# Eight stores of normalised rows moved behind the first block's last gradient store, and the next row tiles loaded one row pair later

## Chip, cores and metric

The kernel runs on one core of a Trainium2 chip. The metric is the device time of one execution in microseconds (us). Engines are named as the profile names them: PE is the matrix engine (its weight loads are PEld), DVE the vector engine, ACT the scalar engine, POOL GpSimd, and SP the engine that issues most of the DMAs. "SPq" marks what SP issues. The clock granted to PE is 1.00 over the whole profile of the kernel before.

## What is computed

The reference is the forward and backward pass of a sum of two branches over a normalised input. With x of 2048 rows by 1024 columns and weights of 1024 by 3584:

```python
xn = layernorm(x)                                   # rows, eps 1e-5
A  = xn * (conv_over_2048_rows(k_shift * v, ssm_k) + k_shift * v * ssm_D)
B  = (relu(xn @ W_gate) * (xn @ W_up)) @ W_down
out = x + A + B
# and the gradients of x, k, v, shift_k, ssm_k, ssm_D, W_gate, W_up, W_down for a given grad_out
```

For branch B the backward pass needs grad_out @ W_down^T (`ps_h` in the kernel), the gradients of gate and up (`ug_d`), and then the weight gradients and the gradient of xn. Everything is bf16 with f32 sums.

## The kernel before, in words

The kernel is one instruction stream per engine, ordered partly by hand and partly by a planner that places each instruction by a priority and by its dependencies. `keep_in_program_order` (through `Pri.pin`, line 32) fixes an instruction's place on its engine. `issue_after(ins)` lets an instruction be placed on its queue only behind another one. Neither adds a wait of its own in the running program.

**Phases.** `hidden` (line 1223) makes gate, up and grad_out @ W_down^T; `grad_down` (1621) and `grad_in` (1660) make the weight gradients; `out_phase` (1709) and `grad_x` (1825) finish the outputs. Beside `hidden` and the weight gradients the convolution branch (`ABranch`) is woven in, a few matrix instructions at a time (`ps_c`, line 83).

**hidden.** The loop over n has 14 passes: 2 halves of 8 row tiles of 128 rows (s = 0 to 7), each against 7 column blocks of 512. A pass is called a block here: the *first block* is n = 0, the second is n = 1. In a block, the row tiles go in pairs (sp = 0, 2, 4, 6). For a pair there are two products for gate (`ps_g`), two for up (`ps_u`) and two for the gradient (`ps_h`), each of eight 128x512 matmuls (`gemm8`, 1151). ACT takes the Relu of gate into a tile `ru` (1281), DVE multiplies with up (1296 or 1299), forms `ht` (1305), and after ACT has copied `ps_h` (1456) DVE makes both gradients in `ru` (1457). `ht` is stored to `h_d` (1310) and `ru` to `ug_d` (1462). `ru` tiles come from a ring of six buffers, `ht` and `gh` from another ring of six, and PSUM has eight banks (`open_left`, 888).

**Weights.** A block needs gate (`wg`), up (`wu`) and transposed down weights (`wdT`), four pieces of 256 KB each. The next block's pieces are loaded while a block runs, into buffers that the present block has finished with (`load_gate`, `load_up`, `load_down`, 1246 to 1267). In the first block `load_gate` runs twice, two pieces at a time. `wdT` comes through a transposing DMA (`row_piece_T`, 1169). All of these go through SP, which issues in order.

**Normalising.** The rows of x are normalised in chunks (`LN_CHUNKS`, 939): tiles 0 to 7 are read by loads 0 to 5, tiles 8 to 15 by loads 6 to 9, two row tiles (512 KB) each. The tiles lie in a ring of five buffers (`a.lnx`, 127), so load 6 overwrites the buffer that holds the normalised rows 0 and 1, load 7 that of row 2, load 8 that of row 3, and load 9 that of rows 4 and 5. Each normalised row tile is stored to `xn_d` (256 KB). The generator `layer_norm` (958) is advanced by `next(ln)`; `chunk()` (1486) advances it by three, which is one of loads 6 to 9 normalised and stored. For rows 0 to 7 the stores are not issued at once: `kept` collects them (1003, 1031) in the order of rows 0, 1, 3, 2, 4, 5, 6, 7, and lines 1526 to 1529 issue the first four behind pair sp = 2 of the first block and the other four behind pair sp = 6. Rows 8 to 15 are stored as soon as they are scaled (line 1001).

**Queues.** In the first block the stores of `h_d` and `ug_d` go through POOL (`nc.gpsimd`), as all `xn_d` stores do; from the second block on `h_d` and `ug_d` go through SP. POOL also makes the index tables for the convolution (`tables`, 149; the last of them is line 226, read by DVE at 227). In the built program the DMAs of SP rotate over eight semaphores and those of POOL over eight others, so each DMA waits until the one eight before it on its side has landed.

**The convolution branch** reads `xn_d` first at line 302 (`load_xn`, issued through line 99 by SP, in fixed order), and that load waits for all sixteen `xn_d` stores, because it reads a column slice of every row.

Of the kernel before, what the change touches and what calls it, by code (L numbers as in the profile page):

```python
# [17 lines left out]
P = 128  # L18
# [30 lines left out]
class ABranch:  # L49
# [47 lines left out]
    def load(self, out, in_):  # L97
        self.pri.now()
        ins = self.nc.sync.dma_start(out=out, in_=in_)
        if self.pin:  # L100
            self.tc.keep_in_program_order(ins)
        else:
            self.pri.pin(ins)
# [776 lines left out]
class LnMlp:  # L880
# [342 lines left out]
    def hidden(self, first, goT, load, ln, tables, Wg, Wu, Wd, g, xn_d, h_d, ug_d):  # L1223
# [6 lines left out]
        for n in range(N):  # L1230
            half, fb = divmod(n, self.FB)
            s0, cols, ahead = half * HS, slice(fb * 512, fb * 512 + 512), n == 0
# [13 lines left out]
            def load_gate():  # L1246
                if last:
                    self.slab_part(h_d, 0, "hs", self.hs, 4, sg)
                elif ahead and nw[0] is None:
                    nw[0] = self.col_block(Wg, nb, "wg", to[0], part=range(2))  # L1250
                    nw.append(self.pieces)
                elif ahead:
                    self.col_block(Wg, nb, "wg", to[0], part=range(2, 4), out=nw.pop())
                else:
                    nw[0] = self.col_block(Wg, nb, "wg", to[0])
# [5 lines left out]
            def load_down(q):  # L1261
                if last and q == 0:
                    self.slab_part(h_d, 0, "hs", self.hs, 0, spare)
                elif not last:
                    if q == 0:
                        nw[2] = []
                    nw[2].append(self.row_piece_T(Wd, nb, "wdT", to[2], q, n == 1))
# [105 lines left out]
            def gate_up(sp):  # L1373
                end = sp == HS - 2
                if ahead and not end:
                    gate(sp)
                    yield from step(self.PACE[0])

                    def turn():
                        flip(sp + 2)  # L1380
                        with self.tc.issue_after(self.copied.ins):
                            chunk()
                    up(sp, None, {4: turn})
                    yield from step(self.PACE[1])
                    gate(sp + 1)
                    yield from step(self.PACE[0])
                    up(sp + 1)
                    yield from step(self.PACE[1])
                    return
                rows = [(f, s) for f in (gate, up) for s in (sp, sp + 1)]  # L1390
                for f, s in sorted(rows, key=lambda r: r[1]) if ahead else rows:
                    f(s)
                    yield from step(self.PACE[f is up])
                    if end and f is gate and s == sp + 1:
                        (load_up if ahead else load_gate)()
                if end and ahead:
                    for q in range(4):
                        load_down(q)
                elif end:
                    load_up()  # L1400
                if swap:
                    next_rows(sp)
# [8 lines left out]
            def last_rows(sp):  # L1411

                self.hold = self.busy = True
                for q in range(2):
                    load_down(sp // 2 + q)

                def run(f, s):
                    f(s)
                    yield from step(self.PACE[f is up])
                yield from run(gate, sp)  # L1420
                yield from run(gate, sp + 1)
                yield from run(up, sp)
                yield from run(gate, sp + 2)
                yield from run(gate, sp + 3)
                load_gate()
                yield from run(up, sp + 1)
                yield from grad_row(sp)
                yield from run(up, sp + 2)
                yield from run(up, sp + 3)
                load_up()  # L1430
                self.busy = swap and not last
                if n == 1:
                    chunk()
                if swap:
                    next_rows(sp)
                    next_rows(sp + 2)
                for s in range(sp + 1, HS):
                    yield from grad_row(s)
                if swap:
                    next_grads(sp)  # L1440
                    next_grads(sp + 2)
# [7 lines left out]
            def grad_row(s, after={}):  # L1449
                ps = self.ps_tile("ps_h")  # L1450
                self.gemm8(ps, gT[s], wd, None, after)

                def finish():
                    gh = self.e1_tile("gh")
                    kept = dict(always=ahead and s == 0)
                    self.pri.pin(nc.scalar.copy(out=gh[:], in_=ps[:]), **kept)  # L1456
                    self.pri.pin(nc.vector.tensor_tensor(out=ru[s][:], in0=ru[s][:], in1=gh[:].rearrange(
                        "p (o f) -> p o f", o=1).to_broadcast([P, 2, 512]), op=ALU.mult), **kept)

                    def store(r=(s0 + s) * P, cols=cols, t=ru[s]):  # L1460
                        queue = nc.gpsimd if n == 0 else nc.sync
                        self.put = queue.dma_start(out=ug_d[r:r + P, :, cols], in_=t[:])
                        self.pri.pin(self.put)
                    self.defer(store)
                if ahead and s == 0:
                    late.append(finish)
                else:
                    finish()
                yield 1730
                self.tick()  # L1470
# [8 lines left out]
            def grad(sp):  # L1479
                for s in (sp, sp + 1):  # L1480
                    at = 3 if sp == 0 else 0
                    yield from grad_row(s, {at: lambda: flip_ahead(sp)} if ahead and s == sp + 1 else {})
                if swap:
                    next_grads(sp)
# [12 lines left out]
            for sp in range(0, HS, 2):  # L1497
                self.pri.now()
                while len(gT) < min(sp + 4, HS):
                    with self.tc.issue_after(self.turned.ins if sp == 4 else self.copied.ins):  # L1500
                        gT.append(self.load_T(g, len(gT), "goT", HS + len(gT)))
                if ahead and sp == 4:
                    with self.tc.issue_after(self.loaded.ins):
                        load_gate()
                if ahead or sp < HS - 4:
                    if not ahead:
                        load_down(sp // 2)
                        yield from gate_up(sp)
                        if n == 4 and sp == 2:
                            for k in filter(self.bare, range(HS)):  # L1510
                                xT[k] = self.load_T(xn_d, k, "xnT", k)
                        if sp:
                            self.hold = False
                        elif fb:
                            self.busy = False
                    if not ahead or sp != 4:
                        yield from grad(sp)
                    if ahead and sp == 2:
                        yield from grad(4)
                elif sp == HS - 4:  # L1520
                    yield from last_rows(sp)
                if ahead:
                    with self.tc.issue_after(self.stored.ins):
                        if sp == 0:
                            load_gate()
                if ahead and sp in (2, 6):
                    with self.tc.issue_after(self.put.ins):
                        for put in self.kept[0:4] if sp == 2 else self.kept[4:8]:
                            put()
                if ahead and sp == 6:  # L1530
                    with self.tc.issue_after(self.sent.ins):
                        load(6)
                if ahead and sp + 4 < HS:
                    yield from gate_up(sp + 4)
                if n == 1 and sp < 4:
                    with self.tc.issue_after(self.stored.ins):
                        for i in ((7,), (8, 9))[sp // 2]:
                            load(i)
                if n == 1 and sp != 4:
                    chunk()  # L1540
                if ahead and sp == 4:
                    with self.tc.issue_after(self.ln_act.ins), self.tc.issue_after(self.ln_dve.ins):
                        tables()
# [477 lines left out]
```

## Time and profile before

| | us |
|---|---|
| three runs | 1851.29, 1855.92, 1854.02 |
| their median | 1854.02 |
| the profiled execution | 1851.31 |
| its span, first to last instruction | 1849.5 |
| PE busy in the span | 1843.3 |
| DVE, ACT, POOL busy | 1118.4, 647.3, 35.0 |
| mean DMA rate over the span | 187 GB/s |

All times of rows below are us from the start of that span. A row of the timeline gives start, duration, engine, source line, operation, output and inputs, how many instructions were merged into it, and in brackets the idle time before it with what ended it. PE rows overlap a little, since a matmul's row of 0.38 us includes its way through the array, while one starts every 0.216 us. DMA rows are the time that the issuing engine spent on issuing, not the transfer.

### The profile page before, as it was taken

Reading aid. Unit: us, or ns where it says so; the run is one execution under the profiler, and the core shown is the slowest. Engines: PE = TensorE matmul, PEld = TensorE weight load, DVE = VectorE, ACT = ScalarE, POOL = GpSimd, SP = SyncE. Lnnn points to the kernel's source line nnn. Section 1 sums busy time; section 2 is a strip of 40 time slices with the busy share of each in tenths; the row PEclk is TensorE's granted clock in tenths of the full one; section 3 lists DMA queues with packets and bytes.
Section 4 is the critical chain, followed back from the end, with each engine's and each line's share of the span. In section 5 each row is a group of like instructions: output and inputs, shape, how many; then the busy total and the mean of one; then the engine's idle time right before and its main releaser. Section 6 shows DMA issues by size and latency. Waiting matters only on the chain.

```text
span 1849.5 us, 32388 instructions
## 1 busy us (share of the span) xinstructions
PE 1843.3 (100%) x13182; PEld 847.7 (46%) x13182; DVE 1118.4 (60%) x1652; ACT 647.3 (35%) x1218; POOL 35.0 (2%) x72
## 2 busy tenths in 40 slices
PE   9999999999999999999999999999999999999999
PEld 5444444444444444444444444444444544444444
DVE  6656797698789758585685667821212222566652
ACT  6644544445444454545544454320000000111100
POOL 2200000000000000000000000000000000000000
PEclk9999999999999999999999999999999999999999
DMA  9997769968767866639567445389999767799963
GB/s 251 273 219 195 172 167 240 209 168 205 186 157 199 243 162 160 166 102 273 130 155 173 142 117 161 105 232 251 256 239 249 181 144 170 173 210 215 207 150 74
DMA packets 749989, 345.97 MB, mean 187 GB/s; under 512 B 581272, under 2 KB 718480, under 8 KB 749840
## 3 DMA queue, kind: packets, MB, share of 16 engines
q1 hardware_dynamic: 736048, 312.18, 71.1%
q10 hardware_dynamic: 9632, 17.04, 3.0%
q0 software_dynamic: 4160, 14.68, 2.4%
q8 instruction: 103, 1.69, 0.4%
q14 instruction: 46, 0.38, 0.1%
HBM read 143.79 MB, written 103.83 MB: 134 GB/s over the span
## 4 chain that ended last, share of the span: by engine, by line
PE 99%; DMA 1%; DVE 0%; issue 0%; DVEq 0%
PE ps_x L1870 21%; PE ps_w L1571 20%; PE ps_h L1153 10%; PE ps_g L1153 10%; PE ps_u L1153 10%; PE ps_o L1738 10%; PE ps_d L1571 9%; PE ps_c L83 4%; PE ps_d L1587 2%; PE ps_w L1587 1%; PE ps_r L1772 0%; DMA wdT<-in_B_W_down_dram 0%; DMA wu<-in_B_W_up_dram 0%; PE ps_g L1327 0%; PE ps_u L1327 0%; PE pst_x L1198 0%
## 5 line engine op out<-in xcount | busy, mean ns | idle before, releaser
L1571 PE MATMUL ps_w<-ugs,xn_nat 128*128 128x512 bf16 x1728 | 381.1, 379 | 0.0
L87 ACT CAST arena<-ps_c 128x512 bf16<-128x512 f32 x576 | 293.8, 611 | 103.8 <-PE ps_c L83 103.6
L1153 PEld LDWEIGHTS <-xnT 128*128 128x128 bf16 x1760 | 168.7, 98 | 205.8 <-issue 6.2
L1571 PEld LDWEIGHTS <-xn_nat 128*128 128x128 bf16 x1728 | 165.4, 98 | 200.7 <-issue 6.1
L343 DVE STREAM_TRANSPOSE arena<-arena 128x1024 f32<-128x1024 f32 x96 | 179.4, 1934 | 112.2 <-ACT arena L87 101.8
L1153 PE MATMUL ps_h<-wdT,goT 128*128 128x512 bf16 x896 | 203.6, 379 | 1.5 <-DMA wdT<-in_B_W_down_dram 1.5
L1153 PE MATMUL ps_u<-wu,xnT 128*128 128x512 bf16 x880 | 202.8, 379 | 0.4 <-DMA wu<-in_B_W_up_dram 0.3
L1153 PE MATMUL ps_g<-wg,xnT 128*128 128x512 bf16 x880 | 201.6, 379 | 0.0
L1870 PE MATMUL ps_x<-wgT,ggT 128*128 128x512 bf16 x896 | 198.6, 379 | 0.0
L1870 PE MATMUL ps_x<-wuT,guT 128*128 128x512 bf16 x896 | 198.6, 379 | 0.0
L1888 ACT ACTIVATE w<-xn,m 128x512 f32<-128x512 bf16 x32 | 24.3, 807 | 480.4 <-DVE m L1881 367.0
L1738 PE MATMUL ps_o<-wd,hT 128*128 128x512 bf16 (+1 forms) x896 | 187.6, 372 | 0.0
L1571 PE MATMUL ps_d<-g_nat,hs 128*128 128x512 bf16 x768 | 169.9, 379 | 0.0
L1870 PEld LDWEIGHTS <-guT 128*128 128x128 bf16 x896 | 87.7, 98 | 105.7
L1870 PEld LDWEIGHTS <-ggT 128*128 128x128 bf16 x896 | 87.7, 98 | 105.5
L1153 PEld LDWEIGHTS <-goT 128*128 128x128 bf16 x896 | 86.7, 98 | 105.9 <-issue 2.8
L1738 PEld LDWEIGHTS <-hT 128*128 128x128 bf16 x896 | 87.7, 98 | 100.0
L1456 ACT CAST gh<-ps_h 128x512 bf16<-128x512 f32 x112 | 66.2, 593 | 184.6 <-PE ps_h L1153 174.1
L1574 ACT CAST wi<-ps_w 128x512 bf16<-128x512 f32 x108 | 64.5, 598 | 187.6 <-PE ps_w L1571 154.9
L1730 DVE TENSOR_TENSOR ya<-ya,xe 128x1024 bf16<-128x1024 bf16 x16 | 11.1, 692 | 175.1 <-DMA xe<-xn_d 175.1
L91 DVE TENSOR_TENSOR t<-arena 128x2048 bf16<-128x2048 bf16 x96 | 113.9, 1219 | 0.4
L1571 PEld LDWEIGHTS <-hs 128*128 128x128 bf16 x768 | 73.3, 98 | 88.3 <-issue 1.8
(152 smaller groups left out, 1426.8 us busy)
## 6 DMA issues: line engine op xcount, KB each, us to landing
ugs<-ug_d SPq DMA_DIRECT2D x112, 256.0 KB, 5.0
ug_d<-ru SPq DMA_DIRECT2D x104, 256.0 KB, 4.2
wu<-in_B_W_up_dram SPq DMA_DIRECT2D x56, 256.0 KB, 4.8
hs<-h_d SPq DMA_DIRECT2D x56, 256.0 KB, 4.9
out_dram<-wi SPq DMA_DIRECT2D x56, 256.0 KB, 4.5
wg<-in_B_W_gate_dram SPq DMA_DIRECT2D x55, 256.0 KB, 4.1
h_d<-ht SPq DMA_DIRECT2D x104, 128.0 KB, 2.0
gt<-in_grad_out_dram SPq DMA_DIRECT2D x32, 256.0 KB, 5.6
```

What stands on the lines that cost most here:

```text
L83: self.pri.pin(self.nc.tensor.matmul(out, lhsT=lhsT, rhs=rhs, start=start, stop=stop))
L87: self.pri.pin(self.nc.scalar.copy(out=out, in_=in_))
L91: self.pri.pin(self.nc.vector.tensor_tensor(out=out, in0=in0, in1=in1, op=op))
L343: self.pri.pin(self.nc.vector.transpose(out=df[:, c0:c0 + 32, :], in_=sf[:, c0:c0 + 32, :]))
L1153: self.pri.pin(self.nc.tensor.matmul(ps[:], lhsT=xT[:, kt * P:(kt + 1) * P], rhs=w(kt), start=(kt == 0), stop=(kt == self.DT - 1)), always ...
L1456: self.pri.pin(nc.scalar.copy(out=gh[:], in_=ps[:]), **kept)
L1571: self.pri.pin(self.nc.tensor.matmul(ps[:], lhsT=lhsT(st), rhs=rhs(st), start=(st == 0), stop=(st == self.ST - 1)))
L1574: self.pri.pin(self.nc.scalar.copy(out=out, in_=ps[:]))
L1587: self.pri.pin(self.nc.tensor.matmul(ps[i][:], lhsT=lhsT(i, st), rhs=rhs(i, st), start=(st == 0), stop=(st == self.ST - 1)))
L1738: nc.tensor.matmul(ps, lhsT=hT[:, kt, :], rhs=self.wd[:, kt, oc], start=(kt == 0), stop=(kt == self.FT - 1))
L1870: nc.tensor.matmul(ps, lhsT=T[:, kt, :], rhs=W[:, kt, oc], start=(i == 0), stop=(i == n - 1))
L1888: nc.scalar.activation(out=w[:, oc], in_=xn[:, oc], func=ACT.Identity, scale=m[:, 7:8], bias=m[:, 6:7])
```

## The change

Four edits, all in `hidden`:

1. The first four stores of normalised rows (rows 0, 1, 3, 2) no longer go out behind pair sp = 2 of the first block. All eight kept stores are issued together, behind pair sp = 0 of the second block, and placed behind the last gradient store of the first block on POOL.
2. Load 6 leaves the end of the first block. It goes where load 7 was; load 7 goes where load 8 was, and loads 7, 8 and 9 share the second place.
3. The four chunks of normalising that were called in the second block behind pairs 0, 2, 6 and inside the last pairs are now called behind pair 2, inside the last pairs, behind pair 6, and behind pair 0 of the third block.
4. The name `first_put` takes the place of `put` for the store that the kept stores go behind.

```diff
                     def store(r=(s0 + s) * P, cols=cols, t=ru[s]):
                         queue = nc.gpsimd if n == 0 else nc.sync
-                        self.put = queue.dma_start(out=ug_d[r:r + P, :, cols], in_=t[:])
-                        self.pri.pin(self.put)
+                        put = queue.dma_start(out=ug_d[r:r + P, :, cols], in_=t[:])
+                        self.pri.pin(put)
+                        if n == 0:
+                            self.first_put = put
                     self.defer(store)
...
-                if ahead and sp in (2, 6):
-                    with self.tc.issue_after(self.put.ins):
-                        for put in self.kept[0:4] if sp == 2 else self.kept[4:8]:
+                if (n, sp) == (1, 0):
+                    with self.tc.issue_after(self.first_put.ins):
+                        for put in self.kept:
                             put()
-                if ahead and sp == 6:
-                    with self.tc.issue_after(self.sent.ins):
-                        load(6)
                 if ahead and sp + 4 < HS:
                     yield from gate_up(sp + 4)
                 if n == 1 and sp < 4:
                     with self.tc.issue_after(self.stored.ins):
-                        for i in ((7,), (8, 9))[sp // 2]:
+                        for i in ((6,), (7, 8, 9))[sp // 2]:
                             load(i)
-                if n == 1 and sp != 4:
+                if (n, sp) in ((1, 2), (1, 6), (2, 0)):
                     chunk()
```

In the built program the order of PE's 26366 instructions is the same before and after. On POOL four stores move down past two `h_d` stores, five table instructions and the last two `ug_d` stores of that block. On SP one 512 KB load moves from ahead of the second block's first `wdT` issue, and the following three shift one place each. On DVE and ACT one chunk's instructions move down by one row pair or more, and the last table's two DVE instructions move behind the first gradient product of the second block.

## The prediction

> **What bounds the kernel now.** First the page: busy times, then the chain of work that ended last.
>
> ```profile
> span 1849.5 us, 32388 instructions
> PE 1843.3 (100%) x13182; PEld 847.7 (46%) x13182; DVE 1118.4 (60%) x1652; ACT 647.3 (35%) x1218; POOL 35.0 (2%) x72
> ...
> PE 99%; DMA 1%; DVE 0%; issue 0%; DVEq 0%
> ```
>
> PE is busy for 1843.3 of 1849.5 us. All that any reordering can win is the other 6.2 us, and part of that is the head and the tail. So the next view is what PE waited for:
>
> ```profile
> PE ps_h L1153 <- DMA wdT<-in_B_W_down_dram: 1.5, 1, 1.5
> PE ps_warm L1214 <- DVE warm L1211: 1.0, 1, 1.0
> PE ps_u L1153 <- DMA wu<-in_B_W_up_dram: 0.3, 1, 0.3
> ```
>
> Columns: total us, times, longest. Two waits for weights, 1.5 and 0.3 us, no wait for ACT or DVE but the warm-up's. The timeline and the chain of waits give their places, and what SP and POOL issued ahead of the first:
>
> ```profile
> 42.01 1.20 POOL L1031 DMA_DIRECT2D xn_d<-ln_x  x2
> 43.09 0.65 POOL L1001 DMA_DIRECT2D xn_d<-ln_x  x1
> ...
> 43.62 0.65 POOL L1031 DMA_DIRECT2D xn_d<-ln_x  x1
> 43.72 3.57 SPq L1144 DMA_DIRECT2D wu<-in_B_W_up_dram  x4
> ...
> 47.38 8.48 SPq L1171 DMA_TRANSPOSE wdT<-in_B_W_down_dram  x4
> ...
> 55.02 2.60 POOL L1001 DMA_DIRECT2D xn_d<-ln_x  x4
> ...
> 59.86 2.32 PE L1153 MATMUL ps_h<-wdT,goT 128*128 128x512 bf16 x10 [1.50 <-DMA wdT<-in_B_W_down_dram]
> ```
>
> ```profile
> 54.38 5.44 DMA wdT<-in_B_W_down_dram
> ```
>
> The second block's first gradient product uses the four `wdT` pieces in turn and stops before the fourth. That piece was issued at 54.38 and landed 5.44 later, at 59.82. PE wanted it at 59.86 - 1.50 = 58.36. It is 1.5 us late.
>
> **The change part by part.** *The four stores taken from 42 to 44 us.* They are 4 x 256 KB = 1.05 MB. What they cost the transfers beside them is in the DMA view of 42 to 50 us (8 us):
>
> ```profile
> q0 software_dynamic: 521, 1.70, 55.6%
> q1 hardware_dynamic: 1592, 1.17, 48.9%
> ...
> xn_d<-ln_x POOLq DMA_DIRECT2D x4, 256.0 KB, 6.0
> wu<-in_B_W_up_dram SPq DMA_DIRECT2D x4, 256.0 KB, 7.0
> ```
>
> Columns of a queue: packets, MB, share of the sixteen engines' time. q0 carries POOL's DMAs, q1 SP's. Together they take 104.5% (packets overlap a little), so the DMA engines are full, and q0's 1.70 MB took 0.556 x 8 = 4.45 us. The moved 1.05 MB is 4.45 x 1.05 / 1.70 = 2.75 us of all engines. Without it the `wu` pieces (7.0 us to land) and the `wdT` pieces behind them move up, by 2.75 us at most.
>
> How much of this reaches the fourth piece depends on its issue. The issues of the first two and of the last two pieces, from the view of this tile:
>
> ```profile
> L1171 SPq DMA_TRANSPOSE wdT<-in_B_W_down_dram x1: 2491/2491/2491, 47.4 to 47.4; - x1
> ```
>
> ```profile
> L1171 SPq DMA_TRANSPOSE wdT<-in_B_W_down_dram x1: 2654/2654/2654, 50.0 to 50.0; - x1
> ```
>
> ```profile
> L1171 SPq DMA_TRANSPOSE wdT<-in_B_W_down_dram x2: 1485/1530/1576, 52.7 to 54.4; - x2
> ```
>
> While the stores drained an issue took 2.5 to 2.7 us, afterwards 1.5 to 1.6. I read the longer ones as back-pressure from the full engines. Ends: if the long issues belong to the transposes themselves nothing moves (0); if both fall to the later pace, each saves about 1.0, so the fourth is issued 1.0 + 1.1 = 2.1 us sooner, at 52.3, and lands by 57.7 (52.3 + 5.44), ahead of the 58.36. Half of that would already take 1.05 of the 1.50 us away. I take the whole wait: **-1.5 us**, between 0 and -1.5. Two reasons: the issues speed up in this very trace as soon as the stores are through, and the landing itself (5.44) gets shorter too with less ahead of it. What comes next is no DMA wait: the block's later gradient products use the same four pieces.
>
> *The eight stores from 55 us.* The first four of the batch go out at the time, and at the pace, at which four already went; the other four follow from about 57.6 us, when the fourth piece has, by the above, all but landed. So they cost that piece nothing; if it is not early, they are no worse for it than the four before. On POOL the batch holds up one table instruction, the last `iota`:
>
> ```profile
> 57.18 0.62 POOL L226 IOTA itB<- 128x32 int32 x1
> ...
> 58.30 0.29 DVE L227 TENSOR_SCALAR itB<-itB,kkB,obB 128x32 int32<-128x32 int32 x1
> ...
> 61.10 0.69 DVE L1457 TENSOR_TENSOR ru<-ru,gh 128x1024 bf16<-128x1024 bf16 x1 [0.53 <-ACT gh L1456]
> 62.01 3.62 PE L1153 MATMUL ps_g<-wg,xnT 128*128 128x512 bf16 x16
> ```
>
> At 2.60 / 4 = 0.65 us a store the batch ends at 55.0 + 8 x 0.65 = 60.2 and the `iota` at 60.8; DVE's line 227, now placed behind the gradient product of 61.10 (59.6 without the wait), then waits some 0.5 us. PE doesn't feel that: it has eight banks, and 8 x 1.73 = 13.8 us of matrix work before it needs one back (3.62 us is the row of two products, which take 3.45 of PE's time).
>
> *Load 6 and SP.* Load 6 now waits for the stores of rows 0 and 1, since it overwrites their buffer.
>
> ```profile
> 59.89 2.04 SPq L1310 DMA_DIRECT2D h_d<-ht  x2
> 62.02 0.40 SPq L951 DMA_DIRECT2D ln_x<-in_A_q_dram  x1
> 62.52 0.67 SPq L1462 DMA_DIRECT2D ug_d<-ru  x1
> ...
> 79.48 0.60 ACT L1281 ACTIVATE ru<-ps_g 128x512 bf16<-128x512 f32 x1 [0.20 <-PE ps_g L1153]
> ```
>
> ```profile
> DMA to landing us min/median/max: 3.2/5.8/9.8
> ```
>
> The last row is for all `xn_d` stores. Row 1 goes out at 55.7 and lands at 61.5 (median) or 65.5 (longest). SP comes to load 6 at 62.0, or 60.5 without PE's wait, and stands there 1.0 us, at most 5. Queued behind it are the `ug_d` stores of the second block's first rows, a `wdT` piece for the third block, and `h_d` stores. The first to miss them is the Relu of row 6 at 79.48, which rewrites row 0's `ru` (ring of six): 62.52 + 0.67 + 5.8 = 69.0, so 10 us of slack. Cost 0.
>
> *Chunks one row pair later.* ACT and DVE lose a chunk at 65 to 73 us and gain one at about 104 to 113. ACT has four passes, about 5 us with their read-outs, in front of two Relus there; PE's list of waits names neither engine, and the 13.8 us of banks are the cover. If that cover were gone it would be under 5 us. Cost 0.
>
> *The last two stores of rows, beside the other wait.* They leave 102.45 for about 112:
>
> ```profile
> 102.45 1.07 POOL L1001 DMA_DIRECT2D xn_d<-ln_x  x2 [8.66 <-DVE ln_x L998]
> ...
> 112.92 0.69 DVE L1457 TENSOR_TENSOR ru<-ru,gh 128x1024 bf16<-128x1024 bf16 x1 [1.14 <-ACT gh L1456]
> ...
> 120.87 1.88 SPq L99 DMA_DIRECT2D xt<-xn_d  x2
> ...
> 126.38 2.83 SPq L1144 DMA_DIRECT2D wg<-in_B_W_gate_dram  x4
> ```
>
> ```profile
> 136.35 1.96 SPq L1144 DMA_DIRECT2D wu<-in_B_W_up_dram  x4
> ```
>
> ```profile
> 141.29 3.01 PE L1153 MATMUL ps_u<-wu,xnT 128*128 128x512 bf16 x12 [0.35 <-DMA wu<-in_B_W_up_dram]
> ```
>
> ```profile
> q0 software_dynamic: 160, 0.52, 14.3%
> ```
>
> The last row is the DMA view of 102 to 112 us: the two stores took 14.3% of 10 us, 1.4 us of all engines. From 113 to 138 us SP issues one DMA after the other, up to the `wu` for which PE waits 0.35 us at 141. The 1.4 us now fall in this stretch. Ends: -0.35 (the wait goes) and +1.4 (all of it is pushed through). I take **+0.4**: PE's 1.5 us move SP's stretch forward with it, as its transfers are released by PE and DVE, and a part of the 1.4 finds room.
>
> **Sum.** 1851.31 (the profiled execution: span 1849.5 and 1.8 around it) - 1.5 + 0.4 = 1850.2. The median of the runs shown lies 2.7 above the profiled one; on it the same -1.1 gives **1852.9 us**.
>
> **Rivals.**
> *A. The wait for the fourth piece stays,* because a transpose's issue has its own pace under any load. For it: the issues of 47.4 and 50.0 are alike although the mixture beside them changes. Against: those of 52.7 and 54.4. Then 0 + 0.4, or no change at all: **1854.0**.
> *B. Slower: SP stands at `xt`.* That load (120.87, or 119.4 with PE's gain) waits for every store of rows. The last two go out at about 112.1 to 112.5, behind line 998, which stands just ahead of the DVE row of 112.92, taken with PE's gain. A landing of up to 6.9 us costs nothing. At the longest seen, 9.8, SP stands for 2.9 us, in the stretch without slack, and the `wu` at its end is later by as much: with the 1.4 us of engine time it is +4.3, less 1.5: +2.8. It decides against the change from a landing of about 8.4 us, where 1.5 are used up. Central price +2.5 against -1.5: **1855.0**.
> *C. Slower: the `iota` behind the eight stores.* If POOL's stores are drawn out by the busy DVE, DVE stands at line 227, ACT at the table's sine behind it, and PE stops when the banks are full, at about 62.0 + 13.8 = 75.8. It decides from (75.8 - 0.6 - 55.0) / 8 = 2.5 us a store. The rows of the stores speak against it, with DVE little busy (42 to 45 us) and hardly ever idle (56 to 60.5 us):
>
> ```profile
> L1031 POOL DMA_DIRECT2D xn_d<-ln_x x3 | 1.8, 654 | 0.0
> ```
>
> ```profile
> L1001 POOL DMA_DIRECT2D xn_d<-ln_x x3 | 2.1, 898 | 0.0
> ```
>
> ```profile
> 51.66 1.93 POOL L209 IOTA itNi<- 128x32 int32 x1
> ```
>
> The means are 654 and 898 ns: at 0.9 the batch ends at 62.2. For it speaks only the last row, an `iota` that took 1.93 us where the one at 57.18, of the same size, took 0.62. Drawn out by the same 3.1, a store takes 2.8 us, the `iota` ends at 55.0 + 22.4 + 0.6 = 78.0 and PE stops for 2.2 us: -1.5 + 2.2 = +0.7, **1854.7**.
> The Trainium skill, "SBUF — State Buffer", section "A bandwidth-pool intuition that's wrong (but worth ruling out)", speaks for C: GpSimd can't write its DMAs' descriptors while DVE holds the port that they share, so a DMA of about 620 ns takes about 3100 ns beside a DVE copy. By that figure, as an estimate, the batch would take 24.8 us. The trace agrees with the 620 ns (654) and not with the 3100 (898).
>
> **How the numbers follow.** Forecast 0.58, A 0.22, B 0.16, C 0.04. The forecast's own range is -1.85 to -0.1 (both waits gone; half the saving and all 1.4 pushed through is near 0): 1852.2 to 1853.9. The runs shown scatter from 1851.29 to 1855.92, more than any case moves them. So the range runs from the lowest run less both waits, 1851.29 - 1.85 = 1849.4, to the highest and B's price, 1855.92 + 1.0 = 1856.9. By over 0.3% (5.6 us, about what a measurement of this kernel can tell from no change) none of the cases moves it: a gain of 5.6 would need nearly all of PE's 6.2 idle us, so faster 0.02; slower 0.03, B or C at several times its price; the same 0.95.
>
> **What would show it.** Right: in the changed profile the waits of PE have no `wdT` row, or one under 0.5 us; the four `wdT` issues from 47 us take under 2 us each; SP shows a short wait at load 6 and PE none. A: the 1.5 us row is still there. B: the wait for `wu` near 140 us is over 2 us and SP waits at line 99 for `xn_d`. C: DVE waits for POOL at line 227 for over 10 us. I am wrong outright if PE's busy time changes by more than 1 us, or if PE waits anywhere after 150 us, where nothing but the order of the moved instructions could have been passed on.

## The result and the profile after

| | before | after |
|---|---|---|
| median of nine runs each, us | 1853.25 (1849.15 to 1856.16) | 1848.77 (1848.40 to 1849.70) |
| ratio of the times, 95% interval | | 0.9977 (0.9967 to 0.9988) |
| the profiled execution, us | 1851.31 | 1848.82 |
| its span | 1849.5 | 1847.0 |

The change makes the kernel faster by 0.23% (0.12 to 0.33%). 1848.77 lies 0.63 us below the range forecast, and 4.1 below the predicted 1852.9. On the profiled executions the difference is 2.5 us, on the medians 4.5: six of these nine runs of before took over 1852 us, and none of after did.

The page of after, its span and its busy times:

```profile
span 1847.0 us, 32177 instructions
...
PE 1827.6 (99%) x12970; PEld 847.1 (46%) x13182; DVE 1118.6 (61%) x1652; ACT 646.7 (35%) x1218; POOL 34.8 (2%) x72
```

PE's busy time seems to have fallen by 15.7 us. It has not: 212 matmul records are missing (12970 beside 13182 weight loads, and before had 13182 of both). What PE waited for, after:

```profile
PE ps_w L1570 <- issue: 2.9, 18, 0.2
PE ps_d L1570 <- issue: 1.9, 12, 0.2
PE ps_warm L1214 <- DVE warm L1211: 1.0, 1, 1.0
...
PE pst_x L1198 <- DVE ln_x L1009: 0.4, 1, 0.4
PE ps_w L1586 <- DMA out_dram<-wo: 0.2, 1, 0.2
```

The many "issue" gaps of 0.2 us, all behind 600 us, are the places of missing records, and so is the one put down to `wo`: each is 0.16 to 0.18 us long, the weight loads of the missing matmuls are there, and the profiles without missing records have no such gap. The `wdT` and the `wu` rows are gone. The timeline of after at the place of the change, the DMA view of 42 to 50 us, and the issues of the `wdT` pieces:

```profile
43.52 1.94 SPq L1144 DMA_DIRECT2D wu<-in_B_W_up_dram  x4
...
45.56 8.80 SPq L1171 DMA_TRANSPOSE wdT<-in_B_W_down_dram  x5
...
56.71 3.62 PE L1153 MATMUL ps_h<-wdT,goT 128*128 128x512 bf16 x16
56.96 2.56 POOL L1001 DMA_DIRECT2D xn_d<-ln_x  x4
...
59.10 0.60 POOL L226 IOTA itB<- 128x32 int32 x1
...
59.85 1.06 SPq L951 DMA_DIRECT2D ln_x<-in_A_q_dram  x1
...
60.16 3.62 PE L1153 MATMUL ps_g<-wg,xnT 128*128 128x512 bf16 x16
...
117.71 1.32 SPq L99 DMA_DIRECT2D xt<-xn_d  x2
...
134.51 3.63 PE L1153 MATMUL ps_g<-wg,xnT 128*128 128x512 bf16 x15
...
141.72 1.09 PE L83 MATMUL ps_c<-arena,FW 64*32 64x128 bf16 x96
```

```profile
q1 hardware_dynamic: 2343, 1.75, 83.1%
q0 software_dynamic: 208, 0.66, 21.8%
...
wu<-in_B_W_up_dram SPq DMA_DIRECT2D x4, 256.0 KB, 5.1
```

```profile
L1171 SPq DMA_TRANSPOSE wdT<-in_B_W_down_dram x1: 1387/1387/1387, 45.6 to 45.6; - x1
L1171 SPq DMA_TRANSPOSE wdT<-in_B_W_down_dram x1: 2942/2942/2942, 47.0 to 47.0; - x1
L1171 SPq DMA_TRANSPOSE wdT<-in_B_W_down_dram x2: 1254/1332/1411, 50.1 to 51.4; - x2
```

POOL's queue moves 0.66 MB in these 8 us (before: 1.70), SP's 1.75 (before: 1.17). The `wu` issues take 1.94 us in place of 3.57, the pieces land after 5.1 us in place of 7.0, and the fourth `wdT` piece is issued at 51.42, 2.96 us sooner than at 54.38 (the fifth of the five belongs to the third block). So the gradient product runs through in one row of 16.

Where the 2.5 us came from is read off the starts of rows that both traces have. The first `ps_g` row of before, at 62.01, stands in the prediction; the later two rows of before are:

```profile
136.37 3.63 PE L1153 MATMUL ps_g<-wg,xnT 128*128 128x512 bf16 x16
...
144.23 1.09 PE L83 MATMUL ps_c<-arena,FW 64*32 64x128 bf16 x96
```

The first `ps_g` row moved from 62.01 to 60.16 (-1.85), the later one, ahead of the `wu` wait, from 136.37 to 134.51 (-1.86), and the `ps_c` row behind that wait from 144.23 to 141.72 (-2.51); the span's end moved by -2.5. At 7.5 us, the second `pst_x` row already stood 0.19 earlier, ahead of anything changed (7.49 and 7.30). So about 0.2 belongs to the head, 1.66 to the wait for `wdT` (1.50 of idle time and 0.16 more around it), 0.66 to the wait for `wu` at 141 us, and nothing to the 1700 us after that.

### The profile page after: what moved, and what is told of

It is laid out like the page before. It is cut to its first block, busy times and chain, and to the rows that moved or that the text cites. A ratio compares the mean times of both kernels' runs of the same rounds, so it can differ in the third digit from the quotient of the medians.

```text
span 1847.0 us, 32177 instructions
## 1 busy us (share of the span) xinstructions
PE 1827.6 (99%) x12970; PEld 847.1 (46%) x13182; DVE 1118.6 (61%) x1652; ACT 646.7 (35%) x1218; POOL 34.8 (2%) x72
## 4 chain that ended last, share of the span: by engine, by line
PE 97%; DMA 1%; issue 1%; SPq 0%; ACT 0%; DVE 0%; DVEq 0%; ACTq 0%
PE ps_x L1869 21%; PE ps_w L1570 20%; PE ps_h L1153 10%; PE ps_o L1737 10%; PE ps_u L1153 10%; PE ps_g L1153 10%; PE ps_d L1570 9%; PE ps_c L83 4%; PE ps_d L1586 1%; PE ps_w L1586 0%; DMA vt<-in_A_v_dram 0%; PE ps_r L1771 0%; DMA wu<-in_B_W_up_dram 0%; DMA out_dram<-wo 0%; DMA out_dram<-gv 0%
## 5 line engine op out<-in xcount | busy, mean ns | idle before, releaser
L1570 PE MATMUL ps_w<-ugs,xn_nat 128*128 128x512 bf16 x1675 | 375.2, 379 | 4.7 <-issue 2.9
```

The source lines that it names most:

```text
L1570: self.pri.pin(self.nc.tensor.matmul(ps[:], lhsT=lhsT(st), rhs=rhs(st), start=(st == 0), stop=(st == self.ST - 1)))
```

## Experiments

**Theory 1:** the 1.05 MB of early stores makes the fourth `wdT` piece late, and that wait is the gain; the kernel before also scatters for this reason. **Rivals:** the later place of load 6 or of the chunks carries the gain; or the scatter of before has another cause, and the gain on the profiled execution is all there is. In all kernels below PE's matrix instructions stand in the order of before, but for the extra ones that are named. Each set of runs has its own runs of the kernel before on the same chip.

### Stores alone, loads and chunks alone, and both kernels again

`e4_before_again` is the kernel before, unchanged.

> The kernel before, unchanged, to see its scatter and another of its executions. Theory 1 (the four early stores make the fourth transposed weight piece of the second block late, by an amount that differs from execution to execution): times again spread over several us, 1849 to 1856, and the profile shows the wait of PE at line 1153 for the weights near 58 us with another length than 1.5 us, while PE idles nowhere else by over 0.5 us after 10 us. Rival (the variable time sits elsewhere, near 120 to 145 us, where the convolution starts): the wait near 58 us is again 1.5 us and what differs lies at the load of the up weights near 141 us. If neither: times within 1 us of each other.

Measured: 1850.43 us (1849.27 to 1851.77, 12 runs). The 35 runs of before that go with this set had a median of 1850.46. The profile of this execution: PE's waits and the fourth piece.

```profile
PE ps_h L1153 <- DMA wdT<-in_B_W_down_dram: 1.5, 1, 1.5
```

```profile
59.30 2.32 PE L1153 MATMUL ps_h<-wdT,goT 128*128 128x512 bf16 x10 [1.55 <-DMA wdT<-in_B_W_down_dram]
```

The wait for `wdT` is there again with the same size. The wait for `wu` at 141 us is not: no row names it. It belongs to one execution, not to the kernel. And the usual time of before is 1850.4, not 1853 or 1854.

`e1_stores_only` moves only the stores: all eight behind the last pair of the first block.

```diff
-                if ahead and sp in (2, 6):
+                if ahead and sp == 6:
                     with self.tc.issue_after(self.put.ins):
-                        for put in self.kept[0:4] if sp == 2 else self.kept[4:8]:
+                        for put in self.kept:
```

> The four early stores go out with the other four, at the end of the first block; loads 6 to 9 and the chunks of normalising stay in their old places (two of the second block's stores pass load 6 on SP, as it now waits for the rows). Theory 1: the whole gain, 1848.5 to 1850.0, spread under 1.5 us, no wait for weights near 58 us. Rival 2 (load 6, sent at 56 us, is what makes the piece late): as before, about 1853 with several us of spread. Rival 3 (the gain comes from the chunks one row pair later, at 65 to 145 us): 1851 to 1853.

Measured: 1853.7 us (1852.8 to 1855.44), ratio 1.0013 (1.0005 to 1.0022). Slower, a miss. The timeline:

```profile
59.64 0.73 SPq L951 DMA_DIRECT2D ln_x<-in_A_q_dram  x1
...
73.67 2.15 SPq L1310 DMA_DIRECT2D h_d<-ht  x2
...
87.44 2.83 SPq L1144 DMA_DIRECT2D wg<-in_B_W_gate_dram  x4
...
94.18 3.03 PE L1153 MATMUL ps_g<-wg,xnT 128*128 128x512 bf16 x12 [1.41 <-DMA wg<-in_B_W_gate_dram]
97.82 0.61 PE L1153 MATMUL ps_u<-wu,xnT 128*128 128x512 bf16 x2 [0.61 <-DMA wu<-in_B_W_up_dram]
```

The wait for `wdT` is gone, as theory 1 wants, but PE now waits 1.4 us for `wg` and 1.5 us (0.61 of it in the last row) for `wu` of the third block. Load 6 goes out at 59.64, in before at 56.0; the chunk that reads it stands where it stood, so DVE comes to its passes late, SP stands at two `h_d` stores that DVE has not yet made (73.67; 70.62 in before), and the `wg` behind them in SP's order is issued at 87.44 in place of 84.64. The stores by themselves remove one wait and make another; no run of the 12 was under 1852.8 us.

`e2_loads_chunks_only` is the other part: loads and chunks as in after, stores as in before.

```diff
-                if ahead and sp == 6:
-                    with self.tc.issue_after(self.sent.ins):
-                        load(6)
...
-                        for i in ((7,), (8, 9))[sp // 2]:
+                        for i in ((6,), (7, 8, 9))[sp // 2]:
...
-                if n == 1 and sp != 4:
+                if (n, sp) in ((1, 2), (1, 6), (2, 0)):
```

> Loads 6 to 9 and the chunks later, as in the changed kernel; the eight stores in their old places. Theory 1: as before, 1853 with a spread of several us, the wait near 58 us still there. Rivals 2 and 3: the whole gain, 1848.5 to 1850.0, with little spread.

Measured: 1849.91 us (1848.88 to 1857.76), ratio 0.9993 (0.9981 to 1.0005). No change that can be told, and the wait is still there:

```profile
60.16 2.32 PE L1153 MATMUL ps_h<-wdT,goT 128*128 128x512 bf16 x10 [1.94 <-DMA wdT<-in_B_W_down_dram]
```

`f3_stores_and_chunks` is `e1` with the chunks one row pair later, and load 6 left at the end of the first block.

> As the run with the stores alone moved, but the chunks of normalising one row pair later too; load 6 stays at the end of the first block. With the stores alone, PE waited 2.9 us near 93 to 101 us for gate and up weights, since load 6 came late, the first chunk held DVE, and SP stood behind DVE. Theory 1: with the chunks later nothing stands behind load 6, and the time is that of the changed kernel, 1848.3 to 1850.0. If it is the order on SP around load 6 that costs (two stores pass it): 1853 to 1854 as with the stores alone.

Measured: 1848.71 us (1848.33 to 1851.83), ratio 0.9989 (0.9980 to 0.9998): the time of after. `f1_after_again`, the changed kernel in the same set of runs:

> The changed kernel, unchanged, again beside the kernel before. In the executions seen so far the kernel before has most times near 1850.4 us and about a third of them at 1852.6 to 1857.7 us; the changed one had nine between 1848.4 and 1849.7. Theory 1 (two effects: the wait of 1.5 us for the weights goes in every execution, and the late executions go with the early stores): all runs within 1848.3 to 1850.0, none above 1852. Rival (the late executions come from the state of the chip, and have nothing to do with the change): a fifth or more of these runs above 1852 too.

Measured: 1848.85 us (1848.49 to 1850.16), ratio 0.9986 (0.9977 to 0.9995); no row for `wdT` or `wu`. The gain is 0.14% here and was 0.23% above, since six of these 24 runs of before took over 1852 us, and six of nine above. So two edits carry the whole gain: the stores take the wait away, the later chunks keep the stores from making a new one. The place of load 6 shows no effect of its own, and the rival that gave it or the chunks the gain falls with `e2`.

### The bytes put back, and doubled

`e3_after_extra_stores` is after with four additional 256 KB stores, to a scratch tensor that nobody reads, where the four stores went out in before. `f2_before_double_stores` is before with four such stores behind the four early ones.

```diff
+                if ahead and sp == 2:
+                    with self.tc.issue_after(self.first_put.ins):
+                        for i, x in enumerate(self.kept_x[0:4]):
+                            nc.gpsimd.dma_start(out=self.scratch[i * P:(i + 1) * P, :], in_=x)
```

> The changed kernel with four additional stores of the same size (1 MB) from the same tiles at the old place, behind pair 2 of the first block, into a scratch buffer that nobody reads. Theory 1: the gain is lost, about 1853 with a spread of several us, and the wait near 58 us is back. If the place of the loads or of the chunks is what matters: 1848.5 to 1850 as in the changed kernel.

Measured: 1850.3 us (1849.48 to 1855.3), ratio 1.0001 (0.9991 to 1.0011). Timeline:

```profile
41.81 2.25 POOL L1534 DMA_DIRECT2D scratch<-ln_x  x4
43.52 3.98 SPq L1147 DMA_DIRECT2D wu<-in_B_W_up_dram  x4
47.59 9.14 SPq L1174 DMA_TRANSPOSE wdT<-in_B_W_down_dram  x5
...
58.90 2.32 PE L1156 MATMUL ps_h<-wdT,goT 128*128 128x512 bf16 x10 [0.73 <-DMA wdT<-in_B_W_down_dram]
```

The bytes alone bring back the slow `wu` issues (3.98; 1.94 in after), the wait, and the time of before. The wait is 0.73 and not 1.5 us here; this execution, at 1849.48, was the fastest of the twelve.

> The kernel before with four more stores of 256 KB, into a scratch buffer that nobody reads, right behind the four early ones. Theory 1: the wait for the fourth piece near 58 us grows from 1.5 us by up to the 2.75 us that 1 MB of stores took of all DMA engines, to 2.5 to 4.3 us: 1851.5 to 1853.5 in the common executions, and more late ones. If the piece's issue has its own pace and the stores' amount does not matter: the wait stays at 1.5 us and the time at 1850.4.

Measured: 1856.21 us (1854.74 to 1857.31, 8 runs), ratio 1.0027 (1.0017 to 1.0038). More than expected. PE's waits, and its stretch by 2 us (columns: us, busy with count, granted clock as a share of PE's full clock, DMA share, GB/s):

```profile
PE ps_h L1156 <- DMA wdT<-in_B_W_down_dram: 3.2, 2, 1.7
PE ps_u L1156 <- DMA wu<-in_B_W_up_dram: 0.7, 2, 0.5
```

```profile
60.00:62.00 2.00, 0.59 (x2) 0.83 1.14 323
62.00:64.00 2.00, 1.62 (x4) 0.50 0.84 164
64.00:66.00 2.00, 2.00 (x6) 0.50 1.16 327
66.00:68.00 2.00, 2.00 (x7) 0.50 1.06 391
```

The waits grew to 3.9 us. What was not expected is the clock: it is halved from behind 61 us to 68 us, 6.8 us in all, and 6 or 7 matmuls run in 2 us where after runs 10 or 11. That costs another 3.4 us.

### Why the kernel before scatters

`f4_before_look` is one more execution of the kernel before, and was one of its long ones.

> Another look at the kernel before. If it is one of its late executions (over 1852 us), theory 1 has the additional time as a longer wait for the fourth transposed piece near 58 us; a rival (found with the stores alone moved) has it as waits for gate and up weights at 93 to 101 us, behind a late load 6, with the wait at 58 us unchanged. If it is a common one (about 1850.4 us): one wait of 1.5 us and no other over 0.6 us after 10 us.

Measured: 1854.38 us. The timeline, the chain, and PE's stretch:

```profile
57.81 0.59 PE L1153 MATMUL ps_h<-wdT,goT 128*128 128x512 bf16 x2 [0.38 <-DMA wdT<-in_B_W_down_dram]
...
62.21 3.88 PE L1153 MATMUL ps_h<-wdT,goT 128*128 128x512 bf16 x10 [3.81 <-DMA wdT<-in_B_W_down_dram]
```

```profile
54.73 7.44 DMA wdT<-in_B_W_down_dram
```

```profile
58.00:60.00 2.00, 0.40 (x2) 1.00 1.20 138
60.00:62.00 2.00, 0.00 (x0) 1.00 1.05 212
62.00:64.00 2.00, 1.79 (x5) 0.50 1.02 394
64.00:66.00 2.00, 2.00 (x8) 0.65 1.18 350
66.00:68.00 2.00, 2.00 (x11) 1.00 1.32 366
```

The fourth piece was issued only 0.35 us later than in the profile of before, but took 7.44 us to land in place of 5.44. PE stood for 3.81 us, and then the clock was halved for 3.4 us: 4.2 us of waits less the usual 1.5, and 1.7 for the clock, are 4.4, and 1850.4 + 4.4 = 1854.8, near the 1854.38 measured. The other waits that the expectation named at 93 to 101 us are not there.

The Trainium skill, "TensorE: Matmul & The Clock Gate", section "HAM oscillation — how this bites in real kernels", names this: "no PE-idle gaps >~3.4µs", or the array falls back to half its clock. This trace agrees (a gap of 3.81 us, then 3.4 us at 0.50). `f2` doesn't: its longest gap was 1.75 us.

Each run's record has its mean granted clock, and 3.4 us at half clock show in it as 0.999. So the runs without a profile can be sorted, too, though for them the longer wait is not seen, only the clock. Of 96 runs of the kernel before beside the experiments, 73 have a clock of 1.000: 1848.72 to 1852.75 us, median 1850.34. The other 23 have 0.999 or 0.998: 1852.62 to 1857.71, median 1854.20. Under 1.000 are also 2 of the 12 runs of `e2`, 3 of 12 of `e3`, 8 of 12 of `e1` (with its own waits), and one of 11 of `f3` (1851.83). All 20 runs of after have 1.000. In the three runs shown ahead of the prediction two were over 1853.

Whether the clock falls because PE stands, or beside it because of the full DMA engines, was tried by giving PE something to do. `g2_before_filled` (and again `g5`) puts 7 matmuls, into a bank that nobody reads, ahead of the fourth piece: additional work of 1.5 us.

```diff
+                if (n, s) == (1, 0):
+                    pf = self.ps_tile("ps_fill")
+
+                    def fill(m):
+                        for _ in range(m):
+                            self.pri.pin(nc.tensor.matmul(pf[:], lhsT=gT[0][:, 0:P], rhs=gT[0][:, 0:512],
+                                                          start=True, stop=True), always=True)
+                    after = {5: lambda: fill(7)}
                 self.gemm8(ps, gT[s], wd, None, after)
```

> The kernel before with 7 extra 128x512 matmuls (1.5 us of PE's time, into a bank that nobody reads) ahead of the second block's fourth weight piece, where PE waits 1.5 us. Theory 1: in most executions the time is as before, about 1850.4 us (within 0.5), since the matmuls take the place of the wait; the late executions (one in four of before's at 1853 to 1858) had a wait of near 3.8 us and 3.4 us of half clock behind it; with 1.5 us of that filled the clock stays, so a late one is at most 2.7 us over the others, 1853.1. Rival 1: late executions come as often and as high as in before, for a reason that has nothing to do with PE standing idle. Rival 2: the matmuls add their 1.5 us in full: 1851.9.

> The same kernel again as the one before with 7 extra matmuls ahead of the fourth weight piece (1850.64 us; all 12 runs at a mean clock of 1.000, one of them at 1854.66 us), for more runs. Theory 1: again no run, or at most one, with a clock under 1.000, where 19 of 78 runs of the kernel before have one. Rival: about one in four, three of twelve.

Measured: 1850.64 us (1850.04 to 1854.66, 12 runs), ratio 0.9997 (0.9988 to 1.0005), and 1850.44 us (1850.17 to 1854.35, 11 runs), ratio 0.9998 (0.9989 to 1.0007). The first one's timeline:

```profile
58.09 1.67 PE L1456 MATMUL ps_fill<-goT 128*128 128x512 bf16 x7
59.85 2.32 PE L1153 MATMUL ps_h<-wdT,goT 128*128 128x512 bf16 x10
```

The 1.5 us of extra work cost nothing, since PE would have stood. All 23 runs have a clock of 1.000. At 23 of 96 some 5.5 were due, and the chance of none is (73/96) to the power of 23, 0.002. The 12 runs of `e4` all have 1.000 too; with them it is 85 of 108, and 0.004. Both take the runs as independent. Two of the 23 were still long (1854.66, 1854.35), above the 1853.1 expected at most, with the full clock; they have no profile, and their cause stays open.

`g1` puts 8 and 7 matmuls into `f2`, but behind the second and third pieces, so behind the wait for the second piece, the longest; `g4` puts 11 and 4 ahead of them (`after = {1: lambda: fill(11), 3: lambda: fill(4)}`); `g3` is `f2` again.

> The kernel before with the four extra scratch stores, unchanged, on the same chip as the one with the 15 matmuls, to compare with it: 1856.2 us again (1854.7 to 1857.3), with two PE waits of 1.4 to 1.8 us and half the granted clock for some us behind them.

Measured: 1856.77 us (1855.47 to 1858.23, 8 runs), clock 0.998 or 0.999 in every run, as in every run of `f2`. The waits are not those of `f2`: 3.81 and 0.56 us.

```profile
61.52 1.01 PE L1156 MATMUL ps_h<-wdT,goT 128*128 128x512 bf16 x2 [3.81 <-DMA wdT<-in_B_W_down_dram]
```

```profile
60.00:62.00 2.00, 0.48 (x2) 0.58 1.12 302
```

With one step down to 0.50, a mean of 0.58 over these 2 us puts the step at 60.3, some 2.6 us after PE's last row ended (57.71) and before the gap was over.

> The kernel before with the four extra scratch stores (1856.2 us, two PE waits of 1.75 and 1.44 us in the second block's first gradient product, then half the granted clock for 6.8 us), and 15 extra 128x512 matmuls (8 and 7, some 3.2 us of PE's time, into a bank that nobody reads) put into that product where PE waited. Theory 1: the half clock comes from PE standing idle, and costs 3.4 us (6.8 us at half speed) on top of the wait. Then PE is busy through the wait, the granted clock stays 1.00 at 60 to 68 us, and the time is about 1852.8 us (1852.2 to 1854). Rival: the clock falls for another reason (the full DMA engines beside it, for one): still 0.50 for some us, and 1856 us or more, up to 1859 if the extra matmuls do not hide in the wait.

Measured: 1857.8 us (1856.62 to 1858.33, 5 runs), a miss: the matmuls came too late to fill the longest wait (still 2.4 us for the second piece, and 1.6 for `wu`) and are up to 3.2 us of work of their own. The clock was 1.000 in three of five runs.

> The kernel before with the four extra scratch stores (1856.2 and 1856.8 us, clock 0.998 to 0.999 in every run), with the same 15 extra matmuls as the run that missed, but now 11 ahead of the second weight piece and 4 ahead of the third, where PE stood in the profiles of that kernel (3.8 and 0.6 us). Theory 1: the half clock follows from PE's standing idle and costs 3.4 us of the 6; the matmuls take the place of the idle time, so the mean granted clock is 1.000 in nearly all runs and the time is 1852.8 to 1853.5 us (1848.8 and a wait of 4.0 to 4.4). Rival 1: the half clock comes with the crowded DMA engines whatever PE does: 0.998 or 0.999 as before, and 1856 us or more. Rival 2: the clock stays but nothing is won, since the time is set by when the weights land: that would need a wait of 7 us in place of 4.

Measured: 1855.44 us (1854.31 to 1857.17, 8 runs). The clock is 1.000 in all 8 runs, where the 16 runs without the matmuls all had less. The timeline:

```profile
7.53 0.59 PE L1330 MATMUL ps_g<-wg,xnT 128*128 128x512 bf16 x2 [0.86 <-DMA wg<-in_B_W_gate_dram]
...
59.13 2.54 PE L1459 MATMUL ps_fill<-goT 128*128 128x512 bf16 x11
62.06 0.59 PE L1156 MATMUL ps_h<-wdT,goT 128*128 128x512 bf16 x2 [0.39 <-DMA wdT<-in_B_W_down_dram]
...
64.72 2.32 PE L1156 MATMUL ps_h<-wdT,goT 128*128 128x512 bf16 x10 [0.39 <-DMA wdT<-in_B_W_down_dram]
```

So the half clock follows PE's standing, and not the load on the DMA engines: that rival falls. The time is a partial miss: 0.8 and 1.3 us less than `f2` and `g3` (medians; the ratio to before is 1.0027, 1.0016 to 1.0037, and that of `g3` 1.0024, 1.0013 to 1.0036, each over its own set's runs) in place of some 3.4. By the ratios, a gain in time is not shown. One reason for the shortfall shows: at full speed PE came to the fourth piece before it had landed (64.72, a wait that `f2` at half clock did not have). Another is in the head of this execution, ahead of anything changed: with 0.86 us of wait for `wg` at 7.5 us among others, its `ps_u` product ahead of the first gradient product starts at 54.69, in `f2` at 53.55, so 1.14 later. From there to the next `ps_u` product (70.33, in `f2` 71.28) it takes 2.09 us less than `f2`. Whether the other seven runs have the same head stays open.

## Why the prediction was wrong

The mechanism was right, and so was its place; the time missed by 4.1 us, for the reason in the fourth point.

- **The four stores, -1.5.** Right: 1.66 on the profiled executions. Shown from four sides: `e1`, `f3` and after lose the wait, `e2` keeps it, `e3` brings it back, `f2` makes it grow. The path was partly another. The prediction had 2.1 us from faster `wdT` issues; the fourth is issued 2.96 us sooner, 1.82 of which is there by the first one (45.56 against 47.38), mostly from `wu` issues that took 1.94 in place of 3.57, and 1.14 from the `wdT` issues. "Under 2 us each" held for three of four; one took 2.94.
- **The eight stores and the `iota`, 0.** Right. Four stores took 2.56 us at 56.96, 0.64 each, the `iota` started at 59.10, and PE has no wait. Rival C falls.
- **Load 6 and the chunks, 0.** Right together, but not one by one: the prediction priced the stores without seeing that load 6 behind them with the chunk left in place costs 2.9 us of waits (`e1`). That load 6 itself would wait a little at SP was wrong: at 59.85 it follows `h_d` stores, and nothing names a row store.
- **The carry-over to the median, the step that failed.** "The median of the runs shown lies 2.7 above the profiled one; on it the same -1.1" took the scatter for something that the change leaves alone. It is made of the very wait that the change removes: in about a quarter of the executions (23 of 96, by their clock; by their times, also two of the three first shown) the wait is longer and half a clock follows, as `f4` shows for one such execution. After keeps neither, so its time is that of an execution without the wait: 1850.34 - 1.5 = 1848.84, against 1848.77 and 1848.85. Of the 4.1 us missed, 3.7 are this step (a base of 1854.02 in place of 1850.34) and 0.4 the next one. For the same reason the range was cut off too high: its lower end took 1851.29 as the lowest that before can do, and 1848.72 was seen later.
- **The `wu` wait at 141 us, +0.4.** Wrong in sign (-0.66 on the profiled executions), and wrong as a term: `e4` shows that the wait is not in every execution of before.
- **Rival B.** At `xt` SP stood for the row stores, as B says: the waits of SP in after have

```profile
SPq L99 <- DMA xn_d<-ln_x: 3.1, 2, 1.7
```

  and `xt` left at 117.71. But 3.1 us there brought PE no wait, so the stretch up to `wu` had more slack than B and the +0.4 gave it. **Rival A** falls with the missing `wdT` row.
- **The chances and the signs.** The gain, 0.23%, is within the 0.3% that had 0.95. Neither sign of "wrong outright" came: PE's busy time and its gaps behind 150 us differ by the missing records alone.

What stays open is why the fourth piece lands after 5.4 us in one execution and 7.4 in the next, and what made two runs with the filled wait long at the full clock.

## What to carry to other kernels

When runs scatter by more than the wait that a change removes, ask first whether the scatter is that wait: profile a long execution, or sort the runs by their mean granted clock, before adding the gain to a median. Transfers that nobody waits for, issued by a quiet engine, still hold up the weights issued beside them by another, and in one queue a moved load needs its reader moved with it. A wait of PE can cost twice: once standing, once at the half clock behind it.

## What was not expected of the hardware

- Half clock came not only after one idle gap of 3.81 us (`f4`) but also in an execution whose longest gap was 1.75 us: in `f2` PE ran 0.59 of the 2 us from 60 to 62, after another gap, and the clock was 0.50 for 6.8 us. In `g3` it fell some 2.6 us into a gap of 3.81.
- With 2.54 and 1.02 us of unused matmuls in the same gaps (`g4`) the mean clock was 1.000 in 8 of 8 runs, against 0 of 16 without.
- The time that an issue takes grows with the transfers beside it for plain loads too, not only for the transposing ones: the four `wu` issues took 1.94 us in after, 3.57 in before and 3.98 in `e3`.
